# Mixed V written to DRAM and gathered with keys on partitions in both pairs of batches, sums of V of the second pair in eight parts, order planned with longer store latencies

## The chip, the cores and the metric

The kernel runs on one core of one Trainium2 chip. The metric is the time on the device in microseconds (us), the median of several runs. The core has five engines that work side by side and wait for each other through semaphores: PE (matrix products, with its weight load PEld), DVE and ACT (element-wise work), POOL and SP (here mainly issuers of DMA transfers). Matrix products go to the eight banks of PSUM, 128 partitions x 512 numbers of 32 bits each, and DVE or ACT has to copy them out ("evict") before a bank can be used again.

## The reference

Four batches, eight heads, 768 tokens in 8 blocks of 96, 64 numbers per head. A softmax-like 8 x 8 matrix P per batch and head mixes the blocks of K and of V; then each block of queries attends to its own mixed block; the result goes through a Fourier mix, a layer norm and a feed-forward network of 2048.

```
for _ in range(5):
    P = exp(P - max(P, -1)); P = P / sum(P, -1); P = P / sum(P, -2)
k_sorted = einsum('bhij,bhjcd->bhicd', P, k_b)
v_sorted = einsum('bhij,bhjcd->bhicd', P, v_b)
attn = softmax(0.125 * q_b @ k_sorted.T)          # per block of 96
x = (attn @ v_sorted).transpose(0, 2, 1, 3).reshape(B, S, H * D)
mixed = real(fft(fft(x, axis=1), axis=2))
u = x + mixed
un = (u - mean(u)) / sqrt(var(u) + 1e-6)
out = u + relu(un @ w_ch1) @ w_ch2
```

## The kernel before

**A planner sets the order.** The kernel doesn't write its instructions in order. `P.add` collects operations with, for each engine that may do it, a cost: how long the engine is taken and how long until the result is there. `P.schedule` (L212) then plays these through, takes on each engine the ready operation of the lowest priority number, gives out the tiles of the pools (`P.pool`, `many`), and the instructions are issued in the order that comes out. Every engine works its own list in order. A change of a cost, a priority or the size of a pool therefore moves instructions on every engine. `aim` gives the operations that lead to the first half of the Fourier mix of batch 0 (`goal`) the first rank by their distance to it. Where PE has nothing to do before that goal, filler products (L1391) are put in, one for each 0.22 us that the plan leaves empty.

**Loads.** `load` (L472) issues a DMA, on POOL's queue if nothing else is said; POOL's loads turn 32-bit numbers into 16-bit ones on the way where source and target differ. A load's landing is planned as its bytes at 400 GB/s behind the earlier ones, plus `DLAT` 2.2, plus `late`. K and Q live in `kq`, eight slots: batches 0 and 3 use slots 0 to 3, batches 1 and 2 slots 4 to 7. Q of batches 2 and 3 is loaded in runs of 64 numbers and transposed by a DMA of SP (L945). The two weight matrices go to `w1sb` and `w2sb`.

**V.** V is handled for pairs of batches: pair 0 is batches 0 and 1, pair 1 batches 2 and 3. `nat[t]` has one partition for each of the pair's 128 (batch, head, block), with 96 x 64 numbers: for pair 0 in the space of the feed-forward's `hr[0]`, for pair 1 in slots 0 to 3 of `kq`. `v_path(t)` makes the sum of V over each block's 96 keys: PE adds up by products with the identity (L693), DVE reduces the last eight (L701); `vb`, `vbn` hold the mean. It then reorders V into `vcx` by d (L678 in pair 0, L726 with the mean taken off in pair 1). `v_mix(t)` multiplies with the block-diagonal P, `bdv16[t]`: 64 products with V as the weights (L742), one for each d, so that the result has the 96 keys on partitions and the 128 (batch, head, block) side by side; in pair 0 a second product takes the mean off (L745). Sixteen evictions (L678) copy it to `vsf`, which has 97 partitions (96 keys and a row of ones) and is what the attention product reads (L1021, `av`). Pair 1 writes the places of pair 0, so each half has to wait until the attention of batch b - 2 has read it.

**Attention and Fourier mix.** `kqt` mixes K by products with `bdk` (L927, evicted to `ks`) and transposes Q (L957, to `qt`); `scores` (L982) is followed by the exponential on ACT (L991, `ex`) and a subtraction of one into `eb` (L1004 on DVE, L1006 on ACT); `eb` has four buffers, zeroed at the start by POOL (L537). `av` (L1021) is followed by a reciprocal (L1033) and a product (L1036) into `rt`. `dft1` folds `rt` on DVE (L1053, L1060, L1069, L1074) and multiplies (L1093 to L1103); `dft2` multiplies again (L1179, L1183, L1168, with the rows `rb` that SP copies, L889), adds (L1190, L1202) into `u`, of which there are six, and normalizes (L1216 to L1242) into `un`; the transpose `ut` is made by PE in batch 0 (L1257) and by SP's DMA later (L1249).

**Feed-forward.** `mlp(b, g)` does 64 products with `w1sb` (L1278, evicted into `hr` by L1290 on ACT or L1287 on DVE) and 48 with `w2sb` (L1299), adds the residual in `u` (L1307) and stores `u`: the first half (g = 0) by SP (L1312 to L1318), the second by POOL through an index (L1322). Only after its store can a `u` be written again.

**The softmax rounds.** The five rounds on P (L606 to L639) work on 32 partitions in a corner of `hr[1]`; `bdv_make` and L654 turn the result into `bdv16`, `bdv32` and `bdk`; `a_path` makes the rows for `rb` from the means.

Of the kernel before, what the change touches and what calls it, by code (L numbers as in the profile page):

```python
# [9 lines left out]
F32 = mybir.dt.float32  # L10
# [8 lines left out]
D = 64  # L19
# [25 lines left out]
GT = 384  # L45


def _consts():
# [56 lines left out]
    vrow = np.zeros((1, 128, D + 1), f16)  # L105
# [9 lines left out]
    def as32(m):  # L115
# [8 lines left out]
                rows=rows, erow=np.tile(erow, (1, 4)), vrow=vrow, pack=pack)  # L124


class Op:
    __slots__ = ("n", "costs", "fn", "preds", "succs", "left", "ready", "prio",
                 "vts", "fresh", "nbytes", "end", "start", "eng", "tag",
                 "crit", "late")  # L130
# [13 lines left out]
class Plan:  # L144
# [14 lines left out]
    def add(self, costs, fn, r=(), w=(), prio=None, nbytes=0, tag="",  # L159
            after=()):  # L160
# [7 lines left out]
        o.preds, o.succs, o.vts, o.fresh = set(after), [], [], []  # L168
        for k in r:
            o.preds.update(self.wr.get(k, ()))  # L170
# [41 lines left out]
    def schedule(self):  # L212
# [48 lines left out]
        while todo:  # L261
# [70 lines left out]
            for s in o.succs:  # L332
                s.left -= 1
                for x in s.costs:
                    s.ready[x] = max(s.ready[x],
                                     o.end + (0.03 if x == e else self.XL))
                if s.left == 0:
                    for x in s.costs:
                        avail[x].append(s)
# [27 lines left out]
def kernel(  # L367
# [22 lines left out]
    def many(name, n, shape, dtype):  # L390
# [18 lines left out]
    vcx = ct("vcx", [128, 128 * D + 2], F16)  # L409
    dtab = vcx[:, 6144:7168].rearrange("p (c w) -> p c w", c=4)  # L410
    lt = vcx[0:97, 7168:7168 + LTW]
    vsf = ct("vsf", [97, 128 * (D + 1)], F16)
    vsb = vsf[:, 0:128 * (D + 1)].rearrange("p (g w) -> p g w", w=D + 1)
    eb4 = ct("eb4", [97, 4, EW], F16)
    P.pool("eb", [eb4[:, n, :] for n in range(4)])
# [14 lines left out]
    many("un", 2, [128, DM], F16)  # L430
# [9 lines left out]
             vcx[:, 7938:8194].bitcast(F32).rearrange(  # L440
# [15 lines left out]
    phl = [hr[1].rearrange("p a b -> p (a b)")[  # L456
        0:32, 64 * n:64 * n + 64].rearrange("p (i j) -> p i j", i=NB)
        for n in range(2)]
    pk, pvh, pvl = [hr[1].rearrange("p a b -> p (a b)")[
        0:32, 1024 * n:1024 * n + 1024].rearrange("p (i x) -> p i x", i=NB)  # L460
        for n in (2, 4, 5)]
    pws = hr[1].rearrange("p a b -> p (a b)")[0:32, 3072:3232].bitcast(F32)
# [9 lines left out]
    def load(dst, src, nbytes, w, prio, eng="POOL", r=(), after=()):  # L472
        e = {"POOL": nc.gpsimd, "SP": nc.sync}[eng]
        c = (0.8, 0.8) if eng == "POOL" else (0.1, 2.3)
        o = P.add({eng: c}, lambda _: e.dma_start(dst, src), r=r, w=w,  # L475
                  prio=prio, nbytes=nbytes, tag="load", after=after)
        o.late = 4.0 if after else 0.0
        return o
# [5 lines left out]

    slot = {}
# [14 lines left out]
    def load_qk(nm, b, hf, prio):  # L500
        after = lns[1:2] if b > 1 else ()
        src = {"k": k, "q": q}[nm]
        if nm == "q" and b in QB:
            for h in range(4):
# [4 lines left out]
                    260000, [("kq", slot[nm, b, hf], h)], prio + 0.01 * h,  # L509
# [4 lines left out]
                 "h (p r) d -> p h (r d)", r=6), 786432,  # L514
# [5 lines left out]
    def load_v(t, hf, prio):  # L520
        load(nat[t].rearrange("p (c d) -> p c d", d=D)[
            :, 48 * hf:48 * hf + 48, :],
            vv[128 * t:128 * t + 128, 48 * hf:48 * hf + 48, :], 1572864,
            [("nat", t, hf)] + (hk(0)[8 * hf:8 * hf + 8] if t == 0 else
                                kqk(2 * hf) + kqk(2 * hf + 1)), prio)
# [10 lines left out]
    for n in range(4):  # L536
        P.add({"POOL": (1.5, 1.6)}, lambda _, n=n: nc.gpsimd.memset(  # L537
            eb4[0:96, n, :], 0.0), w=[("ebz", n)], prio=-4996.9, tag="ebz")
    for n in range(2):
        t_ = P.pools["ks"][n][2]  # L540
        P.add({"POOL": (0.4, 0.5)}, lambda _, t_=t_: nc.gpsimd.memset(
            t_[:, :, 96:128], 0.0), w=[("ksz", n)], prio=-4996.8, tag="ksz")
    P.add({"POOL": (0.6, 0.7)}, lambda _: nc.gpsimd.memset(
        vsb[0:96, :, D:D + 1], 1.0 / XSC), w=["vsz"], prio=-4996.8, tag="vsz")
    P.add({"POOL": (0.1, 0.4)}, lambda _: nc.gpsimd.memset(
        pmt[:, 4:7, DM:DM + 2], 0.0), w=["pmz"], prio=-4996.7, tag="small")
# [3 lines left out]
          w=["smalls"], prio=-4996.6, tag="small")  # L550
# [7 lines left out]
            "o (n s) -> o n s", n=4), 13376),  # L558
        vrow=(vsf[96:97, 0:128 * (D + 1)], cn["vrow"].ap(), 16640),
# [14 lines left out]
    load_qk("k", 0, 0, -5000.0)  # L574
    load_qk("q", 0, 0, -4999.0)
    load_v(0, 0, -4998.0)
    load_v(0, 1, -4997.0)
    load_qk("k", 0, 1, -4996.0)
    load_qk("q", 0, 1, -4995.0)
    load_c("dtab", -4994.0)  # L580
    load_c("lt", -4993.0)
    load_c("cs", 19.0)
    load_c("tab", 20.0)
    for c in range(4):
        load_w1(c, 40.0 + c)
    for hf in range(2):
        load_qk("k", 1, hf, 30.0 + hf)
        load_qk("q", 1, hf, 30.5 + hf)
    for c in range(4):
        load_w2(c, 50.0 + c)  # L590
# [4 lines left out]
    V = nc.vector  # L595

    exps = []

    def sk(c, fn):
        o = P.add(c, fn, r=["pw", "rs"] + hk(1), w=["pw", "rs"], tag="sink")  # L600
# [3 lines left out]
    for it in range(5):  # L604
# [16 lines left out]
        if it == 4:  # L621
            P.add({"DVE": (0.14, 0.21)}, lambda _: V.tensor_tensor(
                phl[0], pw, rs[:, None, :].broadcast_to([32, NB, NB]),
                op=ALU.mult), r=["pw", "rs"], w=["phi"] + hk(1), tag="pk")
# [6 lines left out]
        phl[0][:, :, :, None].broadcast_to([32, NB, NB, 16])),  # L631
        r=["phi"], w=["pk"] + hk(1), tag="pk")
    P.add({"DVE": (0.14, 0.21)}, lambda _: V.tensor_tensor(
        phl[1], pw, phl[0], op=ALU.subtract), r=["pw", "phi"],
        w=["plo"] + hk(1), tag="pk", prio=P.prio + 20)
    for n, d_ in enumerate((pvh, pvl)):
# [5 lines left out]
              r=[("phi", "plo")[n]], w=[("pvh", "pvl")[n]] + hk(1), tag="pv",  # L642
# [7 lines left out]
    P.add(pe(0.45), f, r=["pk", "pack"] + hk(1), w=[bk], tag="psk")  # L650
# [35 lines left out]
    def v_path(t):  # L686
        n3 = nat[t].rearrange("p (c d) -> p c d", d=D)
        psm = Buf("pm", "pf") if t else Buf("pm")
        stage = [i for n in range(4) for i in kqk(n)] if t else hk(0)
        for hf in range(2):  # L690
            def f(_, hf=hf):
                for n in range(6):
                    nc.tensor.matmul(  # L693
                        psm.ap, idh,
                        nat[t][:, 3072 * hf + 512 * n:3072 * hf + 512 * n
                               + 512], start=(hf == 0 and n == 0),
                        stop=(hf == 1 and n == 5))
            P.add(pe(mm(512, 6) * (1.0 if t else 1.2)), f,
                  r=[("nat", t, hf), "pack"] + (
                      stage if t else stage[8 * hf:8 * hf + 8]), w=[psm], tag="psm")  # L700
        P.add({"DVE": (0.6, 0.68)}, lambda _: V.tensor_reduce(  # L701
            vb[:, 0, :], psm.ap.rearrange("p (c d) -> p d c", d=D),
            axis=AX.X, op=ALU.add), r=[psm], w=["vb"], tag="vb")
# [8 lines left out]
        vcd = vcx[:, 0:6144].rearrange("p (d r c) -> p d r c", r=6, c=16)  # L712
        for n in range(8):
            qd, hf = divmod(n, 2)
            dr = slice(16 * qd, 16 * qd + 16)
            src = n3[:, 48 * hf:48 * hf + 48, dr].rearrange(
                "p (c r) d -> p d r c", r=6)
            dst = vcd[:, dr, :, 8 * hf:8 * hf + 8]
            if t == 0:
                P.add({"DVE": dve(768), "ACT": act(768, 0.75)},  # L720
                      lambda e, dst=dst, src=src: copy(e, dst, src),
                      r=[("nat", 0, hf)] + stage[8 * hf:8 * hf + 8],
                      w=[("vcx", n)], tag="vcp")
            else:
                P.add({"DVE": dve(768, 1.0, 0.55)},
                      lambda _, dst=dst, src=src, dr=dr: V.tensor_tensor(  # L726
                          dst, src, vbn[:, dr, None, None].broadcast_to(
                              [128, 16, 6, 8]), op=ALU.subtract),
                      r=[("nat", 1, hf), "vbn"] + stage,
                      w=[("vcx", n)], tag="vcd")  # L730

    def v_mix(t):
        bd = bdv16[t].rearrange("p g i -> p (g i)")
        for n in range(16):
            ps = Buf("pm", "pf")

            def f(_, n=n, ps=ps):
                for dd in range(4):
                    d = 4 * n + dd
                    m = 96 if d == D - 1 else 128  # L740
                    o = ps.ap[0:m, 128 * dd:128 * dd + 128]
                    nc.tensor.matmul(o, vcx[:, 96 * d:96 * d + m], bd,  # L742
                                     start=True, stop=(t == 1))
                    if t == 0:
                        nc.tensor.matmul(  # L745
                            o, vbn[:, d:d + 1].broadcast_to([128, m]), bd,
                            start=False, stop=True)
            P.add(pe(0.46 if t == 0 else 0.24), f,
                  r=[("vcx", i) for i in range(2 * (n // 4), min(
                      8, 2 * ((4 * n + 4) // 16) + 2))] + [("bdv16", t)]  # L750
                  + (["vbn"] if t == 0 else []),
                  w=[ps], tag="vmix")
            P.add({"ACT": (0.68, 0.81), "DVE": (0.65, 0.8)},
                  lambda e, n=n, ps=ps: copy(
                      e, vsb[0:96, :, 4 * n:4 * n + 4],
                      ps.ap[0:96].rearrange("p (d g) -> p g d", d=4)),
                  r=[ps, "vsz"], w=[("vsb", n)], tag="vev")

    def bdv_make():
# [6 lines left out]
        P.add(pe(0.4), f, r=["pvh", "pack"] + hk(1), w=[ps], tag="bdv")  # L766
# [657 lines left out]
```

## Time and profile before

| | us |
|---|---|
| median of 3 runs | 289.15 (288.5 to 289.49) |
| the profiled execution | 289.58 |
| its span in the profile | 287.8 |
| first feed-forward product (L1278) starts | 65.34 |
| first attention product (L1021) starts | 32.6 |
| the 48 last products (L1299) start | 271.51 |

The profile's page gives the busy time of each engine (PE and PEld are the products and the weight loads of one engine), and its groups of instructions give line, engine, operation, `out<-in` by the names of the program, the count, the busy time, the mean duration and the idle time ahead of them with what ended it. The view of windows gives these busy times for stretches of the span, with the number of instructions in brackets, then the clock that PE was granted (1.00 is full speed), the share of the DMA engines and GB/s. The timeline gives start and duration of single instructions; a wait that preceded one stands in square brackets with what ended it. A DMA's time to landing counts from its issue. A busy PE is no proof of work: the filler products count as well.

### The profile page before, as it was taken

How to read it: one execution, taken by the hardware profiler on the slowest of the kernel's cores; microseconds unless marked ns; L12 is line 12 of the kernel's file. 1: busy time of each engine (PE TensorE's matmuls, PEld its weight loads, DVE VectorE, ACT ScalarE, POOL GpSimd, SP SyncE). 2: the span in 40 equal slices, each digit the busy share in tenths (PEclk: the TensorE clock that was granted, in tenths of full speed). 3: DMA queues.
4: the chain of work that ended last, by engine and by line, in shares of the span. 5: the costliest groups of instructions: out<-in, count | busy, mean ns of one | idle time of the engine just before them, and what ended most of it. 6: DMA issues, size and time to landing. Idle time of an engine off the chain costs nothing.

```text
span 287.8 us, 5930 instructions
## 1 busy us (share of the span) xinstructions
PE 270.7 (94%) x2355; PEld 157.0 (55%) x2355; DVE 172.1 (60%) x424; ACT 158.0 (55%) x332; POOL 55.0 (19%) x81
## 2 busy tenths in 40 slices
PE   5999998999999986999999999999999999999991
PEld 2558876555745553554567456445545545545540
DVE  4599999999999974773489654136214415410010
ACT  2589889759689343885378126416704614614600
POOL 8993304150000280001300000021000012000022
PEclk9999999999999999799999999999999999999998
DMA  7999999999010299222102011211121012022002
GB/s 113 218 257 245 214 208 211 220 185 160 9 24 7 44 182 134 60 53 64 69 19 57 0 75 38 56 75 46 41 92 39 20 35 109 21 61 77 10 17 92
DMA packets 42529, 26.33 MB, mean 91 GB/s; under 512 B 30106, under 2 KB 38824, under 8 KB 42500
## 3 DMA queue, kind: packets, MB, share of 16 engines
q0 software_dynamic: 23536, 18.31, 37.7%
q1 hardware_dynamic: 18966, 7.64, 12.1%
q8 instruction: 18, 0.29, 0.4%
q14 instruction: 9, 0.07, 0.1%
HBM read 28.96 MB, written 6.29 MB: 122 GB/s over the span
## 4 chain that ended last, share of the span: by engine, by line
issue 49%; PE 26%; DVE 15%; POOL 4%; DMA 3%; ACT 0%; POOLq 0%; SPq 0%; DVEq 0%
PE bank L1299 5%; PE bank L1278 5%; PE bank L1391 4%; POOL out_dram L1322 4%; DMA out_dram<-u 3%; PE bank L742 2%; DVE rt L1036 2%; PE bank L927 2%; DVE st L1216 1%; PE bank L982 1%; PE bank L745 1%; DVE eb L1004 1%; PE bank L1093 1%; DVE hr L1287 1%; DVE pmt L1053 1%
## 5 line engine op out<-in xcount | busy, mean ns | idle before, releaser
L1290 ACT ACTIVATE hr<-bank 128x384 f16<-128x384 f32 x106 | 52.0, 491 | 81.9 <-PE bank L1278 75.6
L1278 PE MATMUL bank<-ut,w1sb 128*128 128x384 f16 x512 | 94.3, 329 | 0.7 <-DVE hr L1287 0.4
L1299 PE MATMUL bank<-w2sb,hr 128*128 128x512 f16 x384 | 88.5, 379 | 0.0
L1278 PEld LDWEIGHTS <-w1sb 128*128 128x128 f16 x512 | 48.5, 98 | 34.8 <-issue 2.1
L1299 PEld LDWEIGHTS <-hr 128*128 128x128 f16 x384 | 36.7, 98 | 41.3
L1307 DVE TENSOR_TENSOR u<-bank,u 128x512 f32<-128x512 f32 x24 | 16.5, 689 | 58.5 <-PE bank L1299 58.5
L1322 POOL DMA_INDIRECT out_dram<-u,rows x12 | 11.7, 971 | 164.3 <-DVE u L1307 137.5
L991 ACT ACTIVATE ex<-bank 96x384 f32<-96x384 f32 x64 | 28.1, 484 | 1.6 <-PE bank L982 1.2
L1391 PE MATMUL bank<-pack 128*128 128x480 f16 x63 | 18.0, 419 | 3.3 <-DMA pack<-k_pack 3.3
L1190 DVE SCALAR_TENSOR_TENSOR u<-rt,bank 128x512 f32<-128x512 f16 x12 | 8.1, 684 | 18.6 <-PE bank L1183 13.6
L1202 DVE SCALAR_TENSOR_TENSOR u<-rt,bank 128x510 f32<-128x510 f16 x12 | 8.1, 676 | 18.5 <-PE bank L1168 9.5
L1021 PEld LDWEIGHTS <-eb 97*128 97x128 f16 x416 | 15.8, 98 | 4.1 <-issue 1.8
L1006 ACT ACTIVATE eb<-ex,negone 96x384 f16<-96x384 f32 x30 | 17.9, 615 | 0.2
L1021 PE MATMUL bank<-vsf,eb 97*128 97x65 f16 x416 | 16.9, 193 | 0.9 <-DVE un L815 0.4
L475 POOL DMA_DIRECT2D kq<-in_k_dram x8 | 8.0, 995 | 50.5 <-DVE vcx L726 33.9
L1036 DVE TENSOR_TENSOR rt<-bank,rz 128x384 f16<-128x384 f32 x32 | 17.2, 546 | 0.3
L475 POOL DMA_DIRECT2D kq<-in_q_dram x20 | 16.3, 833 | 2.8 <-DVE rz L1033 1.3
L678 ACT CAST vsf<-bank 96x512 f16<-96x512 f32 x19 | 13.9, 793 | 4.6 <-PE bank L742 4.5
L1216 DVE BATCH_NORM_STATS2 st<-u 128x6 f32<-128x512 f32 x24 | 16.1, 685 | 0.3
L982 PE MATMUL bank<-qt,ks 64*128 64x96 f16 x256 | 11.7, 207 | 2.9 <-DVE u L1190 2.5
L1287 DVE TENSOR_SCALAR hr<-bank 128x384 f16<-128x384 f32 x22 | 12.1, 548 | 2.5 <-PE bank L1278 2.3
L1238 ACT ACTIVATE un<-u,nm,ny 128x512 f16<-128x512 f32 x14 | 11.3, 808 | 3.5 <-DMA ut<-un 1.8
(131 smaller groups left out, 330.3 us busy)
## 6 DMA issues: line engine op xcount, KB each, us to landing
kq<-in_k_dram POOLq DMA_DIRECT2D x8, 384.0 KB, 12.5
w1sb<-in_moe_w_ch_dram POOLq DMA_DIRECT2D x4, 512.0 KB, 16.7
w2sb<-in_moe_w_ch_dram POOLq DMA_DIRECT2D x4, 512.0 KB, 19.5
out_dram<-u SPq DMA_DIRECT2D x8, 256.0 KB, 2.0
kq<-in_q_dram POOLq DMA_DIRECT2D x4, 384.0 KB, 8.1
hr<-in_v_dram POOLq DMA_DIRECT2D x2, 768.0 KB, 12.4
kq<-in_v_dram POOLq DMA_DIRECT2D x2, 768.0 KB, 21.2
kq<-in_q_dram POOLq DMA_DIRECT2D x16, 96.0 KB, 8.2
```

The costliest lines, as they stand in the source:

```text
L475: o = P.add({eng: c}, lambda _: e.dma_start(dst, src), r=r, w=w, prio=prio, nbytes=nbytes, tag="load", after=after)
L991: nc.scalar.activation(ex.ap, pss[h2].ap[0:96, 0:384], AF.Exp, scale=SCALE),
L1006: nc.scalar.activation(ed, src, AF.Identity, bias=negone[0:96])
L1021: nc.tensor.matmul(po.ap[:, 65 * T:65 * T + 65], eb.ap[:, e0:e0 + 128], vsf[:, vi:vi + 65], start=(n == 0), stop=(n == len(WIN[T]) - 1), s ...
L1036: P.add({"DVE": (0.45, 0.56)}, lambda _: V.tensor_tensor(rt.ap[:, :, D * h:D * h + D], po3()[:, :, 0:D], rz.ap[:, :, None].broadcast_to([1 ...
L1216: P.add({"DVE": (0.6, 0.69)}, lambda _, u=u, st=st: V.bn_stats(st.ap, u.ap), r=[u], w=[st], tag="bn")
L1278: nc.tensor.matmul(ps.ap[:, 0:GT], w1sb[:, c, 128 * fc:128 * fc + 128], ut.ap[:, c, :], start=(c == 0), stop=(c == 3))
L1290: nc.scalar.activation(hr[g][:, fc, :], ps.ap[:, 0:GT], AF.Relu)
L1299: nc.tensor.matmul(ps.ap, hr[g][:, fc, 128 * tt:128 * tt + 128], w2sb[:, fc, :], start=(fc == 0), stop=(fc == 15))
L1307: V.tensor_tensor(u.ap, ps.ap, u.ap, op=ALU.add),
L1322: st_ = [nc.gpsimd.indirect_dma_start(out.rearrange("b s m -> (b s) m"), bass.IndirectOffsetOnAxis(ap=rows[:, i:i + 1], axis=0), u.ap, None)]
L1391: nc.tensor.matmul(spin.ap[:, 0:480], idh, pack.bitcast(F16))
```

## The change

V of both pairs is now mixed with V as the moving side: `bdv16[t]` is the weights, so the result has (batch, head, block) on partitions, like `nat`, and 12 products of 512 columns do what 64 did (in pair 0 another 12 take the mean off). The reordering into `vcx` is gone. The result is evicted densely into `vm` (`hr[1]` in pair 0, `nat[1]` itself in pair 1), stored to a DRAM tile `vdr[t]` in three column parts for each batch of the pair, and read back from there by three gathers for each batch, which put the keys on partitions: each of the 32 partitions of a gather receives 64 runs of 64 numbers.

```
-        for n in range(16):
+        for n in range(12):
+            r, hf = divmod(n, 2)
             ps = Buf("pm", "pf")
...
+                nc.tensor.matmul(o, bd, n4[:, r, 8 * hf:8 * hf + 8],
+                                 start=True, stop=(t == 1))
+                if t == 0:
+                    nc.tensor.matmul(
+                        o, bd, vbn[:, None, :].broadcast_to([128, 8, D]),
+                        start=False, stop=True)
...
+            P.add({"ACT": act(512), "DVE": dve(512)},
                   lambda e, n=n, ps=ps: copy(
-                      e, vsb[0:96, :, 4 * n:4 * n + 4],
-                      ps.ap[0:96].rearrange("p (d g) -> p g d", d=4)),
-                  r=[ps, "vsz"], w=[("vsb", n)], tag="vev")
+                      e, vm[:, 512 * n:512 * n + 512], ps.ap),
...
+        for hb in range(2):
+            w64 = slice(64 * hb, 64 * hb + 64)
+            for k_ in range(3):
+                cols = slice(2048 * k_, 2048 * k_ + 2048)
+                P.add({"POOL": (0.7, 7.0 if t else 4.5)} if t or hb else {"SP": (0.4, 4.2)},
+                      lambda e, w64=w64, cols=cols:
+                      (nc.gpsimd if e == "POOL" else nc.sync).dma_start(
+                          vdr[t][w64, cols], vm[w64, cols]),
...
+                o = P.add({"POOL": (1.3, 1.3)},
+                          lambda _, k_=k_, w64=w64, cols=cols:
+                          nc.gpsimd.dma_start(
+                              vsb[32 * k_:32 * k_ + 32, w64, 0:D],
+                              vdr[t][w64, cols].rearrange(
+                                  "g (c d) -> c g d", d=D)),
...
+                          tag="vgt", nbytes=690000)
```

In pair 1 the sums of V are no longer made by PE; DVE takes them straight from `nat[1]` in eight parts of eight d each, and takes the mean off in place in two instructions instead of eight. V of pair 1 is loaded in six pieces instead of two.

```
+        if t:
+            for n in range(8):
+                P.add({"DVE": (1.38, 1.48)}, lambda _, n=n: V.tensor_reduce(
+                    vb[:, 0, 8 * n:8 * n + 8],
+                    n3.rearrange("p c d -> p d c")[:, 8 * n:8 * n + 8],
+                    axis=AX.X, op=ALU.add),
...
+        for hf in range(2):
+            def f(_, hf=hf):
+                m = nat[1][:, 3072 * hf:3072 * hf + 3072].rearrange(
+                    "p (c d) -> p c d", d=D)
+                V.tensor_tensor(m, m, vbn[:, None, :].broadcast_to(
+                    [128, 48, D]), op=ALU.subtract)
```

The loads stand in another order: V of pair 0 comes first; the constants of the Fourier mix, the second half of K and Q of batch 1 and the weights are planned behind the issue of the first gathers (`gate`, `behind`); V of pair 1 and K and Q of batch 3 come later. Zeroing `eb`, now six buffers (`NEB`), moves from POOL to DVE (three buffers) and to copies on ACT (three). Rows of `vsf` are 80 numbers wide (`VW`) instead of 65, `un` has three buffers, and the softmax rounds use corners of `rv`, `fo`, `eo` and `rr`, since `hr[1]` holds mixed V.

```
-    load_qk("k", 0, 0, -5000.0)
-    load_qk("q", 0, 0, -4999.0)
-    load_v(0, 0, -4998.0)
-    load_v(0, 1, -4997.0)
+    load_v(0, 0, -5000.0)
+    load_v(0, 1, -4999.0)
+    load_qk("q", 0, 0, -4998.0)
+    load_qk("k", 0, 0, -4997.0)
...
+    gate = gets[0, 0][-1:]
+    for n, nm in enumerate(("dtab", "lt", "cs")):
+        load_c(nm, 25.0 + n)
```

The plan counts on later landings: a `late` of 8.0 instead of 4.0 for K and Q of batches 2 and 3, 600,000 instead of 260,000 bytes for Q in short runs, 4.5 instead of 2.3 for the rows of `rb`, 9.0 instead of 6.0 and 6.0 instead of 4.0 for the transposes by SP, and for the stores of `u`:

```
-            P.add({"SP": (0.1, 2.3)} if g == 0 else {"POOL": (1.2, 3.5)}, f,
+            P.add({"SP": (0.1, 7.0 if b < 2 else 2.6)} if g == 0 else {"POOL": (1.2, 3.7)}, f,
```

In `dft2` the products of the reversed tokens wait in the plan for the last full one before them (`after=[d2last[-1]]`), the second half of each Fourier mix has a slightly later rank, and the rows of pair 1 (`a_path`) rank behind `dft1` of batch 1 instead of ahead of it.

## The prediction

> **What bounds the kernel now.** I read the share of busy time first, then the busy time by stage, then the waits of single instructions in the stages where PE is not full, then the groups of instructions and the DMA by short windows.
>
> ```profile
> span 287.8 us, 5930 instructions
> PE 270.7 (94%) x2355; PEld 157.0 (55%) x2355; DVE 172.1 (60%) x424; ACT 158.0 (55%) x332; POOL 55.0 (19%) x81
> ```
> ```profile
> core 0: us, PE busy (x) PEld busy (x) DVE busy (x) ACT busy (x) POOL busy (x), PEclk, DMA share, GB/s
> 0.00:20.00 20.00, 16.67 (x104) 8.04 (x104) 13.12 (x45) 10.71 (x14) 18.87 (x26) 1.00 1.00 184
> 20.00:65.00 45.00, 41.98 (x664) 31.06 (x661) 43.69 (x124) 38.09 (x81) 15.07 (x21) 1.00 1.24 219
> 104.00:119.00 15.00, 11.03 (x127) 6.57 (x124) 9.94 (x26) 6.54 (x16) 2.87 (x5) 0.89 1.24 127
> 119.00:282.00 163.00, 162.86 (x1100) 88.24 (x1098) 67.36 (x157) 74.05 (x161) 11.95 (x22) 1.00 0.18 50
> ```
>
> There are three regimes. Up to 65 us the feed-forward part has not begun; PE looks busy, but 63 of its matmuls are filler (L1391), and from 20 us on DVE is busy 43.7 of 45 us: DVE sets when the first feed-forward matmul (L1278) starts, at 65.34. After 119 us PE is busy 162.9 of 163 us: there the end is set by PE's work alone. Between them, at 104 to 119, PE has a hole:
>
> ```profile
> 112.72 0.69 DVE L1190 SCALAR_TENSOR_TENSOR u<-rt,bank 128x512 f32<-128x512 f16 x1 [3.69 <-DMA out_dram<-u]
> 113.45 0.35 PE L982 MATMUL bank<-qt,ks 64*128 64x96 f16 x8 [2.45 <-DVE u L1190]
> 114.98 1.44 PE L1278 MATMUL bank<-ut,w1sb 128*128 128x384 f16 x4 [0.43 <-DVE hr L1287]
> 224.34 4.71 PE L1278 MATMUL bank<-ut,w1sb 128*128 128x384 f16 x28
> ```
>
> A tile u can't be rewritten until its store has landed (7.5 us for the last, beside the K and Q loads of batch 3); DVE waits in order, PE behind it, and afterwards four matmuls take 1.44 us where 28 take 4.55 (0.1625 each, 0.65 for four): the clock had dropped. To price the hole I add PE's queue from 65.34 on at the pitches of undisturbed stretches (L1278 0.1625, L1299 0.2156, L982 0.035, L1021 0.031, L742 0.056): the trace runs 3.1 us behind that sum at 104.09 and 9.2 behind it at 118.46. The hole costs 6.1 us. (The whole queue from 65.34 sums to 204.8; 5.6 more are lost elsewhere.)
>
> So the end is: first feed-forward matmul 65.34, then 216.5 to the end of the last one (271.51 + 48 x 0.2156 = 281.86), then 5.9 of residual, store and end (span 287.8); the profiled execution took 289.58, 1.8 more, and the median is 0.4 under it.
>
> **The change, part by part.**
>
> *DVE before the feed-forward.* I take DVE's queue in the new order and price each instruction by its row less 0.08 us (the overlap that neighbours show: L1053 lasts 0.547 and starts 0.47 apart). From the first bdk (L654) to the last ut copy that DVE makes before L1278 the old queue has 119 issues, 43.5 us; the trace took 45.5 (19.52 to 65.0), so 2.0 were waits. The new queue has 98, 40.4 us: eight evictions of mixed V (0.70) become six of 0.57 from dense rows (priced between ACT's 0.575 for 512 and the 0.69 of L1307), 18 subtractions of one become 11 (more go to ACT, whose own queue I sum to 41.4 where DVE needs its copy at 42.6), and three normalizations of batch 1 move behind. With waits in proportion: 42.2.
>
> ```profile
> L678 DVE CAST vsf<-bank 96x512 f16<-96x512 f32 x13 | 9.6, 781 | 0.4 <-PE bank L745 0.4
> L726 DVE TENSOR_TENSOR vcx<-kq,vbn 128x768 f16<-128x768 f16 x8 | 11.6, 1468 | 0.0
> L678 DVE COPY vcx<-hr 128x768 f16<-128x768 f16 x5 | 4.0, 817 | 0.0
> ```
>
> *Its start.* The eight reorderings of V (five of 0.82 on DVE, three of 1.52 on ACT) go. Three zeroings of eb move from POOL to DVE ahead of the softmax rounds: 1.55 each on POOL; a 1024-wide copy on DVE takes 0.60, so 1.0 for 1672, and between 0.6 and 1.55. With the six zero copies on ACT (0.87 each by L639's 1.04 for 1024) the first exponential is at 4.7 instead of 2.84, the fifth, four rounds of 1.76 and 0.4 of interference later, at 12.1 against 11.93. V is loaded first: at the 0.2 MB/us of the old loads its halves land near 8.5 and 12.4 (before 15.9), so PE's sums end at 15.7 (23 fillers to 10.87, 1.29, 11 fillers of 0.203, 1.29), bdv and the transposes follow, and bdk starts at 18.4 instead of 19.52. First feed-forward matmul: 18.4 + 42.2 + 0.3 = 60.9, a gain of 4.4.
>
> *The new road of mixed V.* PE does 24 matmuls of 0.2156 = 5.2 us instead of 128 of 0.056 = 7.2; DVE is the limit there, so this brings nothing by itself. What it adds is a transfer to DRAM and a gather back, which no row shows. Last eviction near 23.8 (18.4 + 1.2 + 0.25 + 3.4 and waits); store issue 0.4 (SP's L475); landing between 2.0 (median of a 256 KB u store) and 7.5 (the one at 105 us), I take 4.0, since the first loads (4.6 MB) end near 26; issue of the gather's 2048 runs on POOL 1.4 (0.54 for a load of 128 runs, 0.84 for one of 768, drawn on; at most the 2.4 of the slowest K load); draining 1.9, by
>
> ```profile
> DMA packets 1046, 0.16 MB, mean 159 GB/s; under 512 B 1002, under 2 KB 1046, under 8 KB 1046
> ```
>
> which is one microsecond (61 to 62) of the 128-byte Q loads; completion 2.0. Sum 33.5. The first attention product is wanted at 18.4 + 15.8 x 1.046 - 0.6 = 34.3. So the road is covered by 0.8 us, and beyond that each microsecond delays everything: behind the product wait DVE's normalization and all of PE's chain. Bounds of its landing: 30 and 45 (7.5 for the store, 2.4, and 11.2, the median of the eight Q loads at 44 to 66).
>
> The Trainium skill, "DMA: Bandwidth & Descriptors", section "Anatomy of one DMA", gives about 2.0 us plus bytes over 436 GB/s; that would make each 262 KB hop 2.6 us, the landing 30.8 and the cover 3.5. The same page's "Specifications" speaks against this change: under 512 B a transfer misses line rate. The row agrees on the direction (0.16 MB/us in 128-byte runs, 0.2 in long ones).
>
> *Loads behind it.* They queue on POOL behind the gathers: half 1's stores (0.8 MB) and constants (1.0 MB, at 0.4 MB/us, the rate of uncast loads near 20 us) 4.5, K and Q 3.8, three gathers 5.6, w1 2.1 MB at 0.205 = 10.2. From 31.5 this drains at 55.6 and lands at 57.6, wanted at 60.9: covered by 3.3. w2 lands near 68, wanted at 77. V of the second pair lands near 75.6, while DVE wants it near 73.
>
> *Nothing by themselves.* Wider rows of vsf, the scratch of the softmax rounds in other tiles, two more eb and one more un add no instruction but the zeroing. On SP the three stores stand ahead of the rows for rb, whose inputs DVE makes only near 33 us; zeroing gone from POOL frees 6.2 us there, which the loads hid (POOL then waits for landings anyway).
>
> *Second pair.* DVE and ACT lose one sum of 0.67, eight of 1.47 and sixteen evictions of 0.79 (25.1) and get eight partial sums (0.82, the strided copy of 768, to 1.47, the strided subtraction; I take 1.4), two subtractions of 1.95 (four L1053; at most 3.6) and twelve evictions of 0.6 (22.3). PE has 12 x 0.2156 instead of 64 x 0.056, and some attention of batch 1 is moved behind: -1.0 + 1.1 = +0.1. The late V and the sums, in front of the residual additions in DVE's queue, give a new stall, 0 to 6, I take 2.5.
>
> *The hole.* In the new order PE's sum puts the first three rewrites of u 11.8, 8.9 and 9.4 us after the residuals of the tiles that they overwrite (the busy landing was 7.5), and the loads of batch 3 are issued only after the second half's stores: I take the 6.1 as gone.
>
> Sum: 60.9 + 216.5 + 0.1 - 6.1 + 2.5 = 273.9; + 5.9 + 1.8 = 281.6; less 0.4 for the median: **281.2 us**. Own range 277 to 285.
>
> **Rivals.**
> 1. *The hole comes back on POOL* (0.17). Six gathers stand between the stores of the second half's u, each u wanted 0.3 to 1.8 us after its store should land. If a gather's issue costs 2.4 instead of 1.4, that is 6 us: 287.2. For it: POOL has one such row. Against: 0.84 for 768 runs.
> 2. *The road is a little late* (0.15). Busy rows, 5.1 (rb) for the store and 8.2 (Q, median) for the gather: 23.8 + 0.4 + 5.1 + 1.4 + 8.2 = 38.9, 4.6 late: 285.8.
> 3. *Slower: the round trip decides* (0.16). Store 7.5, issue 2.4, landing 11.2: 45.3, 11.0 late. PE then idles; after 2.45 us of waiting the trace lost some 2.2 to half pace. 281.2 + 13.2 = 294.4. It makes the kernel slower from a landing at 42.3 on (8 us late). For it: the stores are issued while the first loads still drain. Against: in the row above the runs drain at over 1000 per us, and nothing else is queued then. The Trainium skill, "TensorE: Matmul & The Clock Gate", section "Part 1: The HAM clock gate", puts the drop after an idle window of about 3.4 us; here it shows after less.
> 4. *It doesn't do what it says* (0.04): the start moves nothing because w1 lands at 65; with the hole gone 285.6.
>
> **How the numbers follow.** Forecast 0.48. A measurement tells this kernel from itself to about 0.3% (0.9 us). Under 288.3 lie the forecast, rival 4, most of 1 and 2: 0.78; within 0.9 us of 289.15 0.06; above it rival 3, 0.16. The range of 277 to 290.5 takes in rivals 1, 2 and 4 and leaves out most of 3.
>
> **What would show it.** L1337 (the new line of L1278) starting near 61; DVE without a wait before the first normalization (L1089); no wait on out_dram in L1249 or L1261; if L1089 waits for PE behind a DMA into vsf, rival 2 or 3; if POOL's gathers last over 2 us, rival 1. A landing of the gathers after 42 us makes the forecast wrong in sign.

## The result, and the profile after

| | before | after |
|---|---|---|
| median (runs) | 289.32 (4) | 297.09 (4; 295.39 to 298.33) |
| ratio, with its 95% interval | | 1.027 (1.021 to 1.033) |
| the profiled execution, its span | 289.58, 287.8 | 295.39, 293.6 |
| first feed-forward product starts | 65.34 | 65.24 |
| from there to the end of the last product | 216.5 | 222.7 |

The kernel became 2.7% slower, where 2.8% faster was forecast. One profiled execution used below, that of ux_first, was a slow one, 3.5 us above the median of its run: its waits are read, its span is not. The same parts of the page and the windows of the changed kernel:

```profile
span 293.6 us, 5635 instructions
PE 267.6 (91%) x2194; PEld 149.2 (51%) x2194; DVE 175.1 (60%) x424; ACT 151.0 (51%) x326; POOL 70.7 (24%) x102
```
```profile
core 0: us, PE busy (x) PEld busy (x) DVE busy (x) ACT busy (x) POOL busy (x), PEclk, DMA share, GB/s
20.00:65.00 45.00, 39.60 (x522) 25.39 (x521) 40.73 (x104) 31.98 (x71) 22.47 (x27) 0.96 1.07 212
65.00:105.00 40.00, 39.84 (x315) 23.01 (x315) 32.28 (x63) 22.36 (x51) 9.20 (x11) 1.00 1.33 134
105.00:125.00 20.00, 20.00 (x163) 9.78 (x161) 15.75 (x36) 15.55 (x34) 11.99 (x16) 1.00 0.77 135
125.00:150.00 25.00, 14.16 (x150) 8.66 (x148) 10.08 (x28) 8.62 (x19) 9.72 (x14) 0.80 1.23 151
150.00:282.00 132.00, 131.80 (x928) 72.09 (x925) 59.74 (x142) 59.96 (x133) 6.54 (x12) 1.00 0.19 51
```

Two things are read here. Up to 65 us DVE is no longer full, 40.7 of 45 us where it had 43.7: it waits, and the start has not moved. The hole of PE at 104 to 119 is gone; there is a larger one at 125 to 150. The timeline of the changed kernel shows what ends it (SPq and POOL lines are issues of DMAs):

```profile
109.94 1.21 SPq L1308 DMA_TRANSPOSE ut<-un  x1
115.81 2.52 SPq L1000 DMA_TRANSPOSE qt<-kq  x1
118.43 3.34 SPq L1308 DMA_TRANSPOSE ut<-un  x2
...
114.58 2.21 POOL L803 DMA_DIRECT2D vsf<-vdr  x2
...
118.91 2.17 POOL L803 DMA_DIRECT2D vsf<-vdr  x2
...
123.17 2.18 POOL L803 DMA_DIRECT2D vsf<-vdr  x2
...
127.63 0.69 DVE L1261 SCALAR_TENSOR_TENSOR u<-rt,bank 128x510 f32<-128x510 f16 x1 [3.32 <-DMA out_dram<-u,rows]
...
136.65 2.72 PE L1337 MATMUL bank<-ut,w1sb 128*128 128x384 f16 x8 [10.78 <-DMA ut<-un]
```

PE stands from 125.87 to 136.65 for the last of three transpositions of `ut`. It was issued near 120.0 and landed at 136.5: 16.5 us, where 2.4 is the median of such transpositions in the whole kernel:

```profile
ut<-un SPq DMA_TRANSPOSE x18, 2.4
```

The eight products of this `ut` then take 0.34 each instead of 0.1625. By the sum of PE's queue that the prediction used, the trace loses 12.8 us between 125.06 and 150.01, of which 10.8 are the wait and the rest the lower clock. The view of DMA issues of the same kernel, from 114.5 to 125.5 (the number at the end is the median from issue to landing):

```profile
q0 software_dynamic: 506, 1.65, 80.7%
q1 hardware_dynamic: 1126, 0.28, 28.0%
...
vsf<-vdr POOLq DMA_DIRECT2D x6, 256.0 KB, 16.9
...
out_dram<-u,rows POOLq DMA_INDIRECT x2, 12.4
```

The share of a queue (q0 is POOL's, q1 SP's) is the sum of its packets' times over 16 engines' span. The two add up to 109%: both queues had packets under way in these 11 us. That the DMA engines were full isn't shown by it, for the same sum reaches 2.12 at 75 to 85 us of this trace. What was issued among the second pair's gathers landed late: the `ut` transpositions, and two stores of `u`, without which `u` can't be rewritten. Whether the gathers are the cause is for the runs to say. A landing is told by 16 updates of a semaphore: for the store of `u` issued at 122.1 fourteen had come by 132.0 and the last two came at 135.2 and 137.3, so that some 5 us of this late landing belong to two parts of sixteen; in gath_last (below) all sixteen of each gather come within 1.4 us. Why two parts lag is open. The groups of the changed kernel give the other prices:

```profile
L803 POOL DMA_DIRECT2D vsf<-vdr x12 | 13.0, 1090 | 15.1 <-DMA vdr<-hr 15.1
...
L719 DVE TENSOR_REDUCE vb<-kq 128x8 f32<-128x768 f16 x8 | 11.4, 1465 | 2.2 <-DMA kq<-in_v_dram 2.2
```

### The profile page after: what moved, and what is told of

Same layout as the page of the kernel before. It is cut to its first block, busy times and chain, and to the rows that moved or that the text cites. A ratio compares the mean times of both kernels' runs of the same rounds, so it can differ in the third digit from the quotient of the medians.

```text
span 293.6 us, 5635 instructions
## 1 busy us (share of the span) xinstructions
PE 267.6 (91%) x2194; PEld 149.2 (51%) x2194; DVE 175.1 (60%) x424; ACT 151.0 (51%) x326; POOL 70.7 (24%) x102
## 4 chain that ended last, share of the span: by engine, by line
issue 48%; DMA 19%; PE 16%; DVE 8%; POOL 5%; ACT 1%; POOLq 0%; DVEq 0%
DMA kq<-in_q_dram 9%; PE bank L1358 5%; PE bank L1337 5%; DMA kq<-in_k_dram 4%; DMA out_dram<-u,rows 3%; POOL out_dram L1381 3%; DMA vsf<-vdr 2%; DMA vdr<-hr 2%; PE bank L1149 2%; DVE rt L1092 1%; DVE st L1275 1%; POOL kq L487 1%; PE bank L1237 1%; PE bank L775 1%; DVE eb L1059 1%
## 5 line engine op out<-in xcount | busy, mean ns | idle before, releaser
L1337 PE MATMUL bank<-ut,w1sb 128*128 128x384 f16 x512 | 92.1, 329 | 10.8 <-DMA ut<-un 10.8
L1349 ACT ACTIVATE hr<-bank 128x384 f16<-128x384 f32 x110 | 53.9, 490 | 89.2 <-PE bank L1337 88.1
L1358 PE MATMUL bank<-w2sb,hr 128*128 128x512 f16 x384 | 87.1, 379 | 0.0
L1366 DVE TENSOR_TENSOR u<-bank,u 128x512 f32<-128x512 f32 x24 | 16.5, 688 | 69.4 <-PE bank L1358 69.3
L1381 POOL DMA_INDIRECT out_dram<-u,rows x12 | 11.8, 987 | 143.4 <-DVE u L1366 138.0
L1061 ACT ACTIVATE eb<-ex,negone 96x384 f16<-96x384 f32 x36 | 21.3, 612 | 0.4
L1076 PEld LDWEIGHTS <-eb 97*128 97x128 f16 x416 | 15.1, 98 | 3.4 <-issue 1.0
L803 POOL DMA_DIRECT2D vsf<-vdr x12 | 13.0, 1090 | 15.1 <-DMA vdr<-hr 15.1
L719 DVE TENSOR_REDUCE vb<-kq 128x8 f32<-128x768 f16 x8 | 11.4, 1465 | 2.2 <-DMA kq<-in_v_dram 2.2
L1059 DVE TENSOR_SCALAR eb<-ex 96x384 f16<-96x384 f32 x28 | 10.9, 393 | 2.7 <-ACT ex L1046 2.4
L1467 PEld LDWEIGHTS <-pack 128*128 128x128 f16 x70 | 6.8, 104 | 11.0 <-DMA pack<-k_pack 3.3
L982 PE MATMUL bank<-bdk,kq 128*64 128x128 f16 x192 | 10.0, 226 | 2.1 <-ACT ex L1046 1.1
## 6 DMA issues: line engine op xcount, KB each, us to landing
kq<-in_v_dram POOLq DMA_DIRECT2D x6, 256.0 KB, 18.4
```

What stands on the lines that cost most here:

```text
L1061: nc.scalar.activation(ed, src, AF.Identity, bias=negone[0:96])
L1076: nc.tensor.matmul(po.ap[:, 65 * T:65 * T + 65], eb.ap[:, e0:e0 + 128], vsf[:, vi:vi + 65], start=(n == 0), stop=(n == len(WIN[T]) - 1), s ...
L1337: nc.tensor.matmul(ps.ap[:, 0:GT], w1sb[:, c, 128 * fc:128 * fc + 128], ut.ap[:, c, :], start=(c == 0), stop=(c == 3))
L1349: nc.scalar.activation(hr[g][:, fc, :], ps.ap[:, 0:GT], AF.Relu)
L1358: nc.tensor.matmul(ps.ap, hr[g][:, fc, 128 * tt:128 * tt + 128], w2sb[:, fc, :], start=(fc == 0), stop=(fc == 15))
L1366: V.tensor_tensor(u.ap, ps.ap, u.ap, op=ALU.add),
```

## The experiments

Theory 1 was that the second pair's transfers crowd the DMA engines; its rivals blamed SP's order, the first pair's road, or the planner's new latencies. For the start, theory S1 blamed DVE's waits for the K and Q loads of batch 1. All runs in one table; ratios are to the kernel before on the same chip, "start" is the first feed-forward product, "rest" from there to the end of the last product, both of the profiled execution:

| run | median | ratio (interval) | start | rest |
|---|---|---|---|---|
| no_gather1 | 284.84 | 0.988 (0.982 to 0.994) | 63.8 | 210.7 |
| ux_first | 295.07 | 1.019 (1.011 to 1.027) | 65.5 | - |
| gath_last | 284.06 | 0.985 (0.978 to 0.992) | 65.8 | 211.2 |
| gath_last_ux | 285.11 | 0.989 (0.985 to 0.992) | 65.1 | 212.8 |
| gl_q1 | 281.10 | 0.972 (0.965 to 0.978) | 63.0 | 211.1 |
| pair0_old | 302.26 | 1.043 (1.035 to 1.051) | 77.5 | 219.7 |
| pair1_only | 298.34 | 1.031 (1.024 to 1.038) | 68.1 | 223.3 |
| old_lat | 286.62 | 0.992 (0.988 to 0.996) | 67.4 | 213.1 |
| gl_q1_w65 | 304.52 | 1.053 (1.046 to 1.060) | 74.5 | 222.4 |
| before_lat | 286.95 | 0.995 (0.992 to 0.998) | 66.4 | 213.0 |
| q1_late | 288.00 | 0.996 (0.992 to 1.000) | 63.1 | 218.6 |
| gl_q1b | 284.96 | 0.989 (0.984 to 0.993) | 67.4 | 209.9 |
| p1_frame_q1 | 284.22 | 0.984 (0.978 to 0.990) | 68.0 | 209.6 |
| gl_q1_old | 282.93 | 0.981 (0.976 to 0.987) | 62.7 | 212.4 |

**no_gather1**: `None if t else nc.gpsimd.dma_start(...)` in place of the gather.

> The order is the changed kernel's; only the six gathers of the second pair aren't issued, so that batches 2 and 3 read the first pair's mixed V. Theory 1 (full DMA engines: the second pair's six stores and six gathers, 3.1 MB, run from 109 to 139 us; ut transposes and u stores issued meanwhile land 9 to 16.5 us after issue instead of 2.4 and 2 to 4): PE's wait of 10.8 us before L1337 at 136.6 goes, the slow clock after it too: 297.1 - 10.8 - 1.3 = about 285, and the ut transpose issued near 120 lands within 5 us. Theory 2 (SP's order: a qt transpose that waits for a free qt until 115.8 holds back the last two ut transposes by 5 to 8 us): without gathers the late issue still costs some 2 us of PE: 287.

284.84: no wait for `ut` or a store; the last `ut` transposition before the old place of the hole lands 2.8 us after issue, and PE's longest wait from 60 us on is this:

```profile
PE bank L1076 <- DVE rt L1092: 0.8, 2, 0.6
```

The gathers are needed for the hole.

**ux_first**: on the transposition of Q, `after=uxs[0:3] if (b, hp) == (2, 3) else ()`.

> One edit: on SP the last qt transpose of batch 2's attention stands behind the three ut transposes of batch 1's first half. Theory 2 (SP's order): all three land before the gathers run, no wait of L1337 for ut, 285. Theory 1 (full DMA engines): the ut transposes land by 121 or so, but the second-half u stores still land at 127.5, 137.3 and 139.7, so that DVE waits before L1261 and PE behind it: of the hole's 12 us some 4 to 8 stay: 289 to 293.

295.07, no gain that would fit theory 2, and above theory 1's range. The timeline shows the hole moved on to the next thing behind the gathers, the store of a `u`, with DVE's residual and PE behind it:

```profile
132.09 0.69 DVE L1262 SCALAR_TENSOR_TENSOR u<-rt,bank 128x510 f32<-128x510 f16 x1 [7.59 <-DMA out_dram<-u,rows]
...
134.68 6.82 PE L1338 MATMUL bank<-ut,w1sb 128*128 128x384 f16 x24 [6.45 <-DVE u L1367]
```

**gath_last**: in `mlp`, after the store is planned,

```
+            if (b, g, tt) == (0, 1, 2):
+                for o in gets[1, 0] + gets[1, 1]:
+                    o.behind.add(P.ops[-1])
+                    o.preds.add(P.ops[-1])
```

> One edit: the second pair's six gathers are issued behind the three second-half u stores of batch 0 (SP's order as in the changed kernel). Theory 1: the stores of V (1.6 MB) still go first, the ut transposes issued at 118 to 121 land by 125, the u stores within 5 us; the hole before L1337 near 125 shrinks from 10.8 to under 2. The gathers end near 140 as before. 286 to 289, unless the ut transposes of the second half of batch 1, issued near 131 to 138, now meet the gathers instead (then a hole near 145). Theory 2: the late issue stays, so some 3 us of wait stay: 288 to 290.

284.06, better than the 286 to 289 expected: 13.0 us under the changed kernel from this edit alone, or about 12 by the two ratios, since the kernel before ran 1 us faster on this chip. In the code, `preds` makes a gather wait for the planned store, and `behind` counts from the store's issue and not from its landing. Its issues from 117.5 to 135.5 and its window over the old place of the hole:

```profile
vsf<-vdr POOLq DMA_DIRECT2D x6, 256.0 KB, 7.5
...
out_dram<-u,rows POOLq DMA_INDIRECT x3, 4.4
```
```profile
125.00:150.00 25.00, 24.63 (x207) 13.91 (x207) 11.43 (x28) 9.45 (x22) 14.05 (x17) 1.00 1.36 162
```

The sum of packet times is no smaller (1.36, where the changed kernel has 1.23 in this window), and the last gather lands at 143.4 instead of 139.1, but nothing urgent stands among them. The second half's `ut`, issued from 135.5 on, do land 8.3 to 9.8 us later; PE has other products until 154.7 and doesn't wait for them (its longest wait after 60 us is 0.4).

**gath_last_ux**: both edits.

> Both edits of the two runs beside it. Both theories: no hole near 125; 285 if the second half's ut transposes, issued at 131 to 139 in the plan, do not meet the gathers; if they do (theory 1 with the crowd moved 15 us later), a hole of up to 8 us near 145 and 293.

285.11, the same within the intervals: SP's order is worth nothing once the gathers are out of the way.

**gl_q1**: gath_last, and `P.ops[-1].late += 3.0` after the first K and Q loads of batch 1, `4.0` after the second.

> Gathers of the second pair behind the u stores, as in gath_last, and one more edit: the plan takes the K and Q loads of batch 1 to land 3 us (first half) and 4 us (second half) later, as they did (2.5 and 3.6 us after the plan). Theory S1 (what kept the first feed-forward product at 65.2 instead of 60.9 is DVE's waits, 1.05 and 1.43 us, for these loads, with ACT and PE behind it): the two copies to qr are issued later, the waits go, first feed-forward product near 62.7, 281.3 us. Rival S2 (DVE's own work is longer than I priced it, 43.1 us against 40.4, and the waits only move to another place): start 64.5 to 65.5, 283.5 to 284.5 us.

281.10, start 62.96: S1 holds. These are the waits in the changed kernel's timeline that it removes:

```profile
27.33 0.36 DVE L706 COPY qr<-kq 128x768 f16<-128x768 f16 x1 [1.05 <-DMA kq<-in_q_dram]
...
44.96 0.36 DVE L706 COPY qr<-kq 128x768 f16<-128x768 f16 x1 [1.43 <-DMA kq<-in_q_dram]
```

The runs with this part of DVE's order unchanged agree: start 63.8, 65.1, 65.2 and 65.8 where such waits sum to 0.8 (no_gather1), 2.1 (gath_last_ux), 2.5 (the changed kernel) and 3.1 (gath_last). In old_lat, whose order differs here, the start is 67.4 with 2.6 of them and 2.0 of others. gl_q1 beats both kernels. That it meets the 281.2 forecast for the changed kernel is luck: its start is 2.1 later than the forecast 60.9, and its rest 1.9 shorter than the forecast 213.0.

**q1_late**: the same edit without the gathers moved.

> The changed kernel with the one edit on the K and Q loads of batch 1 (planned 3 and 4 us later); gathers as in the changed kernel. Theory S1: start 63 instead of 65.2 and no wait of DVE for these loads. Theory 1: the crowd of the second pair is the same and comes 2 us earlier with everything else, so a hole of some 10 us for ut or u stays: 293 to 296. Rival (the hole was an accident of a few hundred ns in SP's or POOL's order): under 288.

288.0: the start is right (63.05), the hole is not; PE waits 4.9 us there, not 10. The edit moved the three `ut` ahead of all but one gather, and only the store of a `u` was caught. So 288.0 lies between the two theories: the hole is there, as theory 1 has it, but a start some 2 us earlier halves PE's wait, so its size depends on where the order puts `ut` and the stores:

```profile
127.90 0.69 DVE L1266 SCALAR_TENSOR_TENSOR u<-rt,bank 128x510 f32<-128x510 f16 x1 [5.58 <-DMA out_dram<-u,rows]
...
130.91 6.33 PE L1342 MATMUL bank<-ut,w1sb 128*128 128x384 f16 x24 [4.92 <-DVE u L1371]
```

**old_lat**: 8.0 to 4.0, 600000 to 260000, 4.5 to 2.3, 9.0 to 6.0, 6.0 to 4.0, and the old costs of the stores of `u`.

> The changed kernel with the planner's old latencies for the loads of K and Q of batches 2 and 3, the rows of rb, the transposes by SP and the stores of u. Theory 1: the crowd is the same, a hole of 8 to 14 us for ut or u: 293 to 299. Rival (the longer latencies spoiled the order): 289 or less.

286.62, in the range of the rival (289 or less): theory 1 as I had put it fails here. The traffic is the same, but with these numbers the sums and the mixing of the second pair come some 10 us later in the order: the three `ut` are issued at 109.5 to 112.4 and land within 2.6 us, two of three `u` stores go ahead of all gathers, and PE has no wait over 0.4 us there. From 109 to 135 us the three stores of `u` land in:

```profile
out_dram<-u,rows POOLq DMA_INDIRECT x3, 4.3
```

The crowd does harm only to what is issued into it; the order decides what that is. The longer latencies are a part of the change, so the hole needed both: the gathers, and the order which these latencies gave.

**gl_q1_old**: gl_q1 with the same old latencies.

> gl_q1 with the planner's old latencies for the loads of K and Q of batches 2 and 3, the rows of rb, the transposes by SP and the stores of u. Theory L (the longer latencies are worth something by themselves once the gathers stand behind the stores: the rewriting of u and the uses of ut are planned late enough): here a wait for ut or for a store of u comes back, 283 to 286. Rival (with the crowd gone they are not needed): 279.5 to 281.5.

282.93, 1.8 above gl_q1, between the rival's range (279.5 to 281.5) and theory L's (283 to 286), and the intervals of the two runs touch. The wait that L named, for `ut` or a store, doesn't appear. The start is 62.7 against 63.0, the rest 212.4 against 211.1. Whether the longer latencies are worth something here stays open.

**before_lat**: the longer latencies in the kernel before.

> The kernel before with the longer planned latencies alone. Theory A (they move the rewriting of u away from the stores, so that the hole of 6.1 us at 104 to 119 goes): 282 to 284. Theory B (they only make the plan wait for landings that come sooner, and move other work late): 289 to 296; no wait for the store of a u over 1 us, but PE waits elsewhere.

286.95, between the two ranges: the rest is 213.0 instead of 216.5, the start comes 1.1 later. So the latencies alone take 3.5 us off the rest of the kernel before; of the 6.1 that the prediction put down to the change as a whole, that much needs no new road for V.

**pair0_old** and **pair1_only**: one pair through DRAM alone.

> The changed kernel with the second pair as in the kernel before (sums by PE, reordering by DVE, 64 products, no DRAM) and the planner's old latencies; four eb, two un, rows of 65 as before. Theory 1 (the second pair's stores and gathers crowd the DMA engines): no wait for ut over 2 us; the old hole of 6 us at the rewriting of u may come back: 284 to 290. Rival (the first pair's road through DRAM costs the time): 293 or more.

> The kernel before with the second pair alone through DRAM (sums by DVE, six stores, six gathers) and the planner's old latencies elsewhere. Theory 1: the crowd comes with it; a wait of 8 to 13 us of PE for ut, or of DVE for the store of a u, between 115 and 150: 293 to 299. Rival (the first pair's part or the longer latencies did it): 286 to 290.

302.26 and 298.34. I can't use these for the question that they were made for: both had rows of `vsf` of 130 bytes for want of room, and in pair0_old the first attention product waited 7.37 us for these gathers (in gl_q1_w65, below, with the same rows, 4.81):

```profile
41.25 2.30 PE L1146 MATMUL bank<-vsf,eb 97*128 97x65 f16 x39 [7.37 <-DMA vsf<-vdr]
```

pair1_only does show theory 1's wait, DVE 15.3 us for a store of `u` and PE 9.6 behind it, but with slower gathers than the changed kernel's, so the size says nothing.

**gl_q1_w65**: gl_q1 with `VW = 65`.

> gl_q1 with rows of vsf of 65 numbers (130 bytes apart) as in the kernel before instead of 80 (160 bytes). Theory W (runs of 128 bytes written to rows 130 bytes apart drain slower: with such rows three gathers of the first pair landed 4.8 and 2.6 us after each other in pair0_old, with 160 bytes 1.9 and 2.0 in the changed kernel): the third gather lands near 41 instead of 35.3, the first feed-forward product starts at 68 to 70 instead of 63, the second pair's gathers end near 150; 288 to 295. Rival (the width is nothing by itself, as my prediction had it): 281 to 282.

304.52, 23.4 us more than gl_q1 for a width. Issues of the second pair's gathers, gl_q1 first, then gl_q1_w65, and two waits of the latter's PE:

```profile
vsf<-vdr POOLq DMA_DIRECT2D x6, 256.0 KB, 7.6
```
```profile
vsf<-vdr POOLq DMA_DIRECT2D x6, 256.0 KB, 13.8
```
```profile
40.84 2.30 PE L1081 MATMUL bank<-vsf,eb 97*128 97x65 f16 x39 [4.81 <-DMA vsf<-vdr]
...
61.20 0.88 PE L1081 MATMUL bank<-vsf,eb 97*128 97x65 f16 x13 [4.26 <-DMA vsf<-vdr]
```

The six land 1.85 us after each other with 160 bytes and 3.96 with 130.

**gl_q1b**: the second K and Q loads of batch 1 ahead of the three constants.

> gath_last; the first K and Q loads of batch 1 planned 3 us later, and the second ones issued ahead of the three constants of the Fourier mix, so that they land 2.4 us earlier. Theory S1: these loads land at 40 to 42.5, the constants at 45, before the 47 at which they are wanted; start 62 to 63.5; 280 to 282. Rival (the constants become the late ones: PE waits for cs before its first Fourier product): start 65, 284.

284.96, a miss of both: the plan, told of an earlier landing, put the copy earlier still, and DVE waited longer for it:

```profile
42.47 0.36 DVE L711 COPY qr<-kq 128x768 f16<-128x768 f16 x1 [3.06 <-DMA kq<-in_q_dram]
```

**p1_frame_q1**: gl_q1 with the first pair's V as in the kernel before.

> gl_q1 with the first pair as in the kernel before (reordering of V by DVE and ACT, 64 + 64 products, 16 strided evictions, nothing through DRAM; the reordered V lies in hr[1]); all else as gl_q1, rows of 160 bytes, six eb. Theory S1 with the first pair's road worth something: its start is that of the kernel before, 65 to 67, 3 us behind gl_q1's 63, and the rest equal: 284 to 286. Rival (the road brings nothing at the start, since DVE sets it either way): start 63 to 64, 281 to 282.

284.22, start 68.0 against 63.0: the first pair's road is worth 5.1 us at the start, where about 3 was expected, and 3.1 in the median. The start lies above the expected 65 to 67, the rest (209.6) 1.5 below gl_q1's.

## Why the prediction was wrong

The profiled execution was forecast at 281.6 and took 295.39, 13.8 more: +4.3 at the start, +12.8 for the hole, -2.5 for a stall that didn't come, and -0.8 in the rest and the tail.

- *The hole* is the step that failed: "I take the 6.1 as gone". The old hole did go: PE was busy 20.00 of 20 us at 105 to 125. A larger one took its place, for which the sum had no term. I had checked the distance of each rewriting of `u` from its store against the busiest landing of the old trace (7.5), and charged the gathers to POOL for their issue alone. No term said what 3.1 MB of stores and gathers do to a DMA issued beside them: with them the stores of `u` took 9.5 to 15.2 and a `ut` 16.5; without them (no_gather1) or with them behind the stores (gath_last) the hole isn't there. Rival 1 had the place, POOL between the stores, with the wrong price: an issue took 1.09, below my 1.4. gath_last shows the size: its rest took 211.2, against 213.0 forecast. Part of the 6.1 belongs to the longer latencies alone (before_lat).
- *The start*: the first bdk came at 17.9 (forecast 18.4). The step that failed is DVE's queue, 42.2 "with waits in proportion". Its waits were 4.27 and not 1.8; 2.48 of them were for two K and Q loads that the old order had not met, and gl_q1 without these starts 2.3 earlier. Its work was 42.8 and not 40.4: rows less 0.08 are too cheap for the subtractions of one (0.33 each against 0.27), the copies to `qr` (0.36 against 0.25) and the evictions of mixed V (0.63 against 0.57). These three make some 1.5 of the 2.4; the remainder isn't accounted for, and all of it is read from the trace, not tried. That the road itself brings some 4 us was right (p1_frame_q1: 5.1).
- *The road of mixed V*: right. Issue 1.09, drain 1.9, the third gather at 34.9 (forecast 33.5), no wait of PE for it: rivals 2 and 3 did not come.
- *Loads behind it*: w1 landed at 59.6 (forecast 57.6) without a wait. V of the second pair landed at 80.9 (75.6) and DVE waited 2.2 for it, but PE had work: no stall.
- *Second pair on DVE*: 1.465 a sum (forecast 1.4) and 1.76 a subtraction (1.95), right.
- *Nothing by themselves*: the wider rows stood in this list. They are worth 23.4 us in gl_q1; I had counted their instructions and not how the gathers write to them. The others of this list (more buffers of `eb` and `un`, the other scratch corners) were not tried alone.

## What to carry to other kernels

A new transfer has three prices: its issue, its landing, and what it does to the landings of those issued among it; the last is read by asking, for each DMA that someone waits for, what stands ahead of it on all queues at that time. Where the total can't shrink, issue the urgent ones first: here that was four lines and 12 to 13 us. And in an order fixed by a plan, a load planned too early stops a busy engine (here for 1.05 and 1.43 us) for work that nobody needed yet.

## What the hardware showed that I had not expected

- Runs of 128 bytes written to rows 130 bytes apart drained at half the rate of rows 160 bytes apart (3.96 against 1.85 us for 256 KB). Other widths weren't tried, so whether a boundary or the odd offsets decide is open.
- In the changed kernel each `u` store landed 0.4 to 0.7 us after the gather issued before it (126.8 and 127.5, 136.9 and 137.3, 139.1 and 139.7): POOL's queue worked in order. SP's queue advanced beside it, slowly. The Trainium skill, "DMA: Bandwidth & Descriptors", section "Queues, rings and completion order", has each DMA engine take turns between queues by whole packets; the two queues' shares above, 80.7% and 28.0% at once, fit that, and don't show it packet by packet.
- After the wait of 10.8 us PE's next eight products took 2.72 us, half pace. Short waits go with a lower clock too: over 45 to 50 us of the changed kernel, with a wait of 1.43 us before L1149 at 47.3, the granted clock was 0.76, and over 20 to 65 us it was 0.96; in gl_q1, without the two waits of DVE, it was 1.00 over 20 to 65 us.
